# Batch 0 of a linear attention brought into the token-major form of the other batches, with the denominator put in the a factor, and a new hand order of the whole kernel

## The chip, the cores and the metric

The kernel runs on one core of one Trainium2 chip. The metric is the device time of one launch in microseconds (us), the median of several runs. The core has a matmul engine (PE, with its weight loads shown as PEld), a vector engine (DVE), a scalar engine (ACT), a general engine (POOL) and an engine that only issues transfers (SP). ACT and POOL can issue transfers too. Each engine works through its own list of instructions in the order in which the program wrote them, and waits at an instruction until what it reads is there.

## The reference: what is computed

Four batches of four heads, 1088 tokens of 32 dimensions each. Queries and keys are projected by S1 and S2 to two factors a and b of 8 numbers, whose outer product is a feature vector of 64. Attention is linear in these features; then comes a layer of width 2048 over all 4352 tokens.

```python
def phi(x):
    a = np.einsum('rd,bhsd->bhsr', S1, x)
    b = np.einsum('rd,bhsd->bhsr', S2, x)
    return np.einsum('bhsi,bhsj->bhsij', a, b).reshape(*x.shape[:-1], r * r)
q_p, k_p = (phi(q), phi(k))
kv = np.einsum('bhsf,bhsd->bhfd', k_p, v)
z = np.sum(k_p, axis=2)
num = np.einsum('bhsf,bhfd->bhsd', q_p, kv)
den = np.einsum('bhsf,bhf->bhs', q_p, z)[..., None] + 1e-06
attn = num / den
...
h = x @ w_in                                  # x: 4352 x 128, the heads side by side
g = h * (1.0 / (1.0 + np.exp(-beta * h)))
out = g @ w_out                               # 2048 -> 128
```

## The kernel before, in words

**The layer (W and V).** beta is multiplied into w_in (`prep_win`, L272) and 1/beta into w_out (`prep_wout_act`, L289, on ACT), so that a plain Silu does for g. The tokens go in ten chunks (`tok_chk`, L61: two of 256, seven of 512, one of 256). `w1` (L344), called W here, does one *wave* of a chunk: two matmuls of 512 tokens, or four of 256, into one of two PSUM tiles (L354), and one Silu of 128x1024 on ACT (L363) that writes g. `w2` (L318), called V, multiplies a g by its part of w_out and adds up in PSUM (L328); with a chunk's last wave DVE turns the sum (L338) and it is stored (L308). There are 68 waves, eight in a chunk of 512 and four in one of 256. V always takes the oldest g that no V has taken yet (`second`, L376), so by how many waves V lags behind W is set by the order in which both are called.

**Attention.** k and q are turned by DVE (L389 and L395) to have the dimension on the partitions. For batches 1 to 3 the work is *token-major*: `kps` and `qps` (L423, L428) project by S1 and S2 on PE, DVE turns the result back to tokens (`turn_ab`, L433), outer products on POOL and DVE make the features (`outer`, L447), `kv` (L498) sums v times features on PE over nine tiles, the features of k are summed to z on DVE (`sum_z`, L557) and added by matmuls on ones (`zs_mm`, L546). kv and z are spread on ACT and turned on PE (`nd_pe`), the features of q are turned by DVE (`turn_qo`, L460), `den_g` (L644) and `num_g` (L656) give denominator and numerator on PE, DVE inverts and spreads the denominator (`invert`, `spread_rc`, L585 to L598) and multiplies while it writes x (`divide_g`, L670). Batch 0 goes another way, in two pieces A and B: `spread` (L469) has PE project q with each a and b repeated so that a plain product (`mult`, L490) gives the features already turned, and z comes from a small Gram matrix of a and b (`gram`, L511, `gram_terms`, `gram_z`).

**Start.** The tiles of S1 and S2 and beta are loaded on ACT's queue (L102, L106), all the rest on SP's, in the order L167 to L179. Eleven matmuls on a constant tile keep PE at work meanwhile (L186).

**Order.** Every engine's list follows one list of short names, written by hand (`SEQ`, L850 on). In it W is `first` (L372), which makes a wave only if its tokens' x is written, and V is `second`, which does nothing without a g. What is left after the list is done by `rest(3)` (L380) with V three waves behind W. The PSUM tiles: two for waves (also used by projections and num), a double one ("two"), two single ones ("one", and "moeout", which holds V's sum; some chunks use "one" for it).

Of the kernel before, what the change touches and what calls it, by code (L numbers as in the profile page):

```python
# [14 lines left out]
P = 128  # L15
# [3 lines left out]
def kernel(  # L19
# [23 lines left out]

    NJK = 9
    TH = T // 2
    TPAD = 4 * NJK
    TCH = 512
    assert T == 34


    q_chk = [(0, 8), (16, 9)]
    QW = 32 * 9

    QB = [0, 9, 16, 25]
    JW = 32 * NJK
    JR = [(0, 2), (2, 4), (4, 6), (6, 9)]
    JR0 = [(0, 2), (2, 4), (4, 6), (6, 8), (8, 9)]
    WARM0 = 11
    NU = NJ // 2
# [7 lines left out]
    sbG = ctx.enter_context(tc.tile_pool(name="sbG", bufs=14))  # L67
# [23 lines left out]


    beta4 = sb([P, DFF // 4], F32, "beta4")
    beta_pu = sb([P, 2, NU], F32, "beta_pu")
    w_in_sb = sb([P, DFF], F32, "w_in_sb")
    w_out_sb = sb([P, NJ, P], F32, "w_out_sb")
    idle = sb([P, P], F16, "idle")
    nc.vector.memset(idle, 1.0)  # L98
    sr = []
    for n, s_ in enumerate((S1, S2)):  # L100
        t = sb([P, D], F32, f"sr{n}")
        nc.scalar.dma_start(  # L102
            out=t, in_=bass.AP(tensor=s_.tensor, offset=s_.offset, ap=[[0, P // R], [D, R], [1, D]])
        )
        sr.append(t)
    nc.scalar.dma_start(  # L106
        out=bass.AP(
            tensor=beta4.tensor,
            offset=beta4.offset,
            ap=[[32 * beta4.ap[0][0], 4], [1, DFF // 4]],  # L110
        ),
        in_=moe_beta.rearrange("(r c) -> r c", r=4),
    )
    nc.gpsimd.dma_start(
        out=beta_pu,
        in_=bass.AP(
            tensor=moe_beta.tensor, offset=moe_beta.offset, ap=[[NU, P], [P * NU, 2], [1, NU]]
        ),
    )
    k_t, q_t, v_t = {}, {}, {}  # L120

    def load_rows(src, dst, b, tag, parts=((0, T),)):
        if b not in dst:
            dst[b] = ld.tile([P, T, D], F32, tag=tag, name=tag)
        for t0, t1 in parts:
            nc.sync.dma_start(
                out=dst[b][:, t0:t1, :],
                in_=bass.AP(
                    tensor=src.tensor,
                    offset=src[b, 0].offset + t0 * D,  # L130
                    ap=[[T * D, P], [1, (t1 - t0) * D]],
                ),
            )


    def load_v(b):
        t = v_t[b] = ld.tile([P, H, NJK, D], F32, tag="v", name="v")
        if b == B - 1:
            nc.gpsimd.memset(t[96:, :, NJK - 2 :, :], 0.0)
        for g in range(4):  # L140
            nj = NJK if b < B - 1 else min(NJK, T - NJK * g)
            nc.sync.dma_start(
                out=t[32 * g : 32 * g + 32, :, :nj],
                in_=bass.AP(
                    tensor=v.tensor,
                    offset=v[b, 0].offset + NJK * g * D,
                    ap=[[T * D, 32], [S * D, H], [1, nj * D]],
                ),
            )

    def load_win(c0, c1):
        nc.sync.dma_start(out=w_in_sb[:, c0:c1], in_=moe_w_in[:, c0:c1])

    def load_wout(i):
        nc.sync.dma_start(
            out=w_out_sb[:, NU * i : NU * i + NU, :],
            in_=bass.AP(
                tensor=moe_w_out.tensor,
                offset=moe_w_out.offset + i * NU * P * P,
                ap=[[NU * P, P], [1, NU * P]],  # L160
            ),
        )

    K_PARTS = ((0, 18), (18, T))
    QA0 = 2 * q_chk[0][1]
    load_rows(k, k_t, 0, "k", K_PARTS)
    load_rows(q, q_t, 0, "q", ((0, QA0),))  # L167
    load_v(0)
    load_win(0, DFF // 2)
    load_wout(0)  # L170
    load_rows(q, q_t, 0, "q", ((QA0, T),))
    load_win(DFF // 2, DFF)
    load_rows(k, k_t, 1, "k")
    load_wout(1)
    load_rows(q, q_t, 1, "q")
    load_v(1)
    load_rows(k, k_t, 2, "k")
    load_rows(q, q_t, 2, "q")
    load_v(2)  # L179


    kvz0 = pso.tile([P, TCH], F32, tag="moeout", name="kvz")

    def keep_warm(n, fresh=False):
        for _ in range(n):
            nc.tensor.matmul(  # L186
                out=kvz0[:, P:],
                lhsT=idle,
                rhs=cut(idle, [[0, 3], [1, P]]),
# [5 lines left out]
    ones = sb([P, P], F32, "ones")  # L195
    nc.vector.memset(ones, 1.0)
    silu0 = sb([P, 1], F32, "silu0")
    nc.scalar.activation(out=silu0, in_=ones[:, :1], func=ACTF.Silu)
    ident = sb([P, P], F32, "ident")
    make_identity(nc, ident)  # L200

    hm = sb([P, 2, R], F32, "hm")
    nc.vector.memset(hm, 0.0)
    for h in range(H):
        nc.vector.memset(hm[32 * h : 32 * h + 32, h % 2, :], 1.0)
    gm = sb([P, 4], F32, "gm")
    nc.vector.memset(gm, 0.0)
    for c in range(4):
        nc.vector.memset(gm[32 * c : 32 * c + 32, c : c + 1], 1.0)
    e3 = sb([P, 3], F32, "e3")  # L210
    nc.vector.memset(e3, 0.0)
    nc.vector.memset(e3[:, 1:2], 1.0)

    mk = sb([P, H, R], F32, "mk")
    nc.gpsimd.tensor_tensor(
        out=mk,
        in0=cut(ident, [[2 * R, H], [1, R]]),
        in1=cut(ident, [[2 * R, H], [1, R]], 64),
        op=mybir.AluOpType.add,
    )  # L220

    kT2, qT2 = [], []
    for n in range(2):
        qT2.append(sb([P, T, 32], F32, f"qT{n}"))
        kT2.append(sb([P, TPAD, 32], F32, f"kT{n}"))
        nc.gpsimd.memset(kT2[n][:, T:, :], 0.0)
    zb0 = sb([P, H, 32], F32, "zb0")
    nc.gpsimd.memset(zb0, 0.0)
    zbg = []
    for n in range(2):  # L230
        t = sb([P, H, 2, 32], F32, f"zbg{n}")
        nc.gpsimd.memset(t, 0.0)
        zbg.append(t)

    keep_warm(WARM0, True)

    sk = sb([P, 2, 2, R], F32, "sk")
    skc = sk.rearrange("p m n r -> p (m n r)")
    sab = []


    def prep_s(n):
        st_ = sb([P, 4, R], F32, f"st{n}")
        nc.vector.transpose(out=st_.rearrange("p u r -> p (u r)"), in_=sr[n])
        nc.gpsimd.tensor_tensor(out=sk[:, :, n, :], in0=st_[:, :2, :], in1=hm, op=MUL)  # L245
        t = sb([P, R, R], F32, f"s{n}")
        nc.scalar.copy(out=t, in_=cut(st_, ([[1, R], [0, R]], [[0, R], [1, R]])[n]))
        sab.append(t.rearrange("p i j -> p (i j)"))


    beta_bc = sb([P, DFF], F32, "beta_bc")

    def beta_half(i):
        t = two("betaps")
# [3 lines left out]
        PS["beta", i] = t  # L258

    def beta_copy(i):  # L260
        nc.scalar.copy(  # L261
            out=beta_bc[:, 1024 * i : 1024 * i + 1024],
            in_=PS["beta", i].rearrange("p a b -> p (a b)"),
        )

    winp = sb([P, NJ, P], F16, "winp")
    woutp = sb([P, NJ, P], F16, "woutp")
    rbeta = sb([P, NJ], F32, "rbeta")

    given = set()  # L270

    def prep_win(j0, n, eng):  # L272
        for j in range(j0, j0 + n):
            given.add(j)
        i, u = divmod(j0, NU)
        o = i * (DFF // 2) + u
        eng.tensor_tensor(  # L277
            out=winp[:, j0 : j0 + n],
            in0=cut(w_in_sb, [[1, n], [NU, P]], o),
            in1=cut(beta_bc, [[1, n], [NU, P]], o),  # L280
# [3 lines left out]
    def prep_rbeta():  # L284
        nc.vector.reciprocal(out=rbeta, in_=beta_pu.rearrange("p i u -> p (i u)"))

    scaled = set()

    def prep_wout_act(j):  # L289
        scaled.add(j)  # L290
        nc.scalar.activation(  # L291
            out=woutp[:, j, :], in_=w_out_sb[:, j, :], func=ACTF.Copy, scale=rbeta[:, j : j + 1]
        )

    xT = sb([P, NTOK], F16, "xT")


    ALT = {len(tok_chk) - 3, len(tok_chk) - 1}
    moe = {"ci": 0, "w": 0, "ready": 0, "acc": None, "todo": []}
# [18 lines left out]
    def w2(ci, j0, jn, g):  # L318
# [6 lines left out]
        for jj in range(jn):  # L325
# [4 lines left out]
                lhsT=woutp[:, j, :],  # L330
# [13 lines left out]
    def w1():  # L344
        ci = moe["ci"]
        t0, tw = tok_chk[ci]
        per = TCH // tw
        jn = 2 * per
        j0 = moe["w"] * jn
        wv = psm.tile([P, 2, TCH], F32, tag="wave", name="wave")  # L350
        for jj in range(jn):
            assert j0 + jj in given
# [3 lines left out]
                lhsT=winp[:, j0 + jj],  # L356
# [5 lines left out]
        gw = per * tw  # L362
        nc.scalar.activation(out=g[:, :, :gw], in_=wv[:, :, :gw], func=ACTF.Silu)  # L363
# [8 lines left out]
    def first():  # L372
        if moe["ci"] < len(tok_chk) and sum(tok_chk[moe["ci"]]) <= moe["ready"]:
            w1()

    def second():  # L376
        if moe["todo"]:
            w2(*moe["todo"].pop(0))

    def rest(lag):  # L380
        while moe["ci"] < len(tok_chk):
            w1()
            if len(moe["todo"]) > lag:
                second()
        while moe["todo"]:
            second()

# [13 lines left out]
    PS, KP, QO, QT, QP, ND, KAB, QAB, ASB, KVZ, KVD, RB = ({} for _ in range(12))  # L401

    def wave2(name):
        return psm.tile([P, 2, 512], F32, tag="wave", name=name)

    def two(name):
        return ps2.tile([P, 2, 512], F32, tag="two", name=name)

# [484 lines left out]
```

## Time and profile before

| what | us |
|---|---|
| median of 3 runs | 116.27 (116.01 to 116.77) |
| profiled execution: span, the only time given for it | 111.9 |
| median less span | 4.4 |
| first W starts | 22.18 |
| x of batch 0 complete | 32.1 |
| W's start of the last 21 waves | 87.33 |
| ACT's 68 Silus, sum of busy time | 65.0 |
| ACT's 16 scalings of w_out | 5.3 |
| PE's matmuls of W and of V, sums of busy time | 39.4 and 37.3 |

The span runs from the first instruction to the last. The profile names an instruction by engine and line; L354 is W, L363 the Silu, L328 V. The mean time of one matmul there holds its whole way through the array; back to back, two of 512 columns take 0.43 us in the chain that ended last. An idle time is put down to the instruction that ended it. The granted clock of PE is given as a share of full speed: it is 1.00 in the first 7 us, changes between 0.5 and 1.0 up to 21 us, and is 1.00 from there.

### The profile page before, as it was taken

How to read it: one execution, taken by the hardware profiler on the slowest of the kernel's cores; microseconds unless marked ns; L12 is line 12 of the kernel's file. 1: busy time of each engine (PE TensorE's matmuls, PEld its weight loads, DVE VectorE, ACT ScalarE, POOL GpSimd, SP SyncE). 2: the span in 40 equal slices, each digit the busy share in tenths (PEclk: the TensorE clock that was granted, in tenths of full speed). 3: DMA queues.
4: the chain of work that ended last, by engine and by line, in shares of the span. 5: the costliest groups of instructions: out<-in, count | busy, mean ns of one | idle time of the engine just before them, and what ended most of it. 6: DMA issues, size and time to landing. Idle time of an engine off the chain costs nothing.

```text
span 111.9 us, 2866 instructions
## 1 busy us (share of the span) xinstructions
PE 100.7 (90%) x1167; PEld 47.9 (43%) x1167; DVE 70.2 (63%) x131; ACT 77.0 (69%) x99; POOL 35.2 (32%) x42
## 2 busy tenths in 40 slices
PE   6539998889999999989999999999899799999950
PEld 3214446234576643333564433344444344444630
DVE  3345727697796998999979779799919320020210
ACT  0503324697997796199899637689983599999930
POOL 5404928996995000070392007600000000000000
PEclk9985955799999999999999999999999999999999
DMA  3989999996002550007601471410150006014054
GB/s 91 298 160 287 415 419 244 253 292 130 18 5 40 78 179 6 0 7 108 187 0 17 60 182 40 74 26 0 15 81 4 0 0 94 6 18 64 15 82 59
DMA packets 22900, 11.33 MB, mean 101 GB/s; under 512 B 19028, under 2 KB 21092, under 8 KB 22888
## 3 DMA queue, kind: packets, MB, share of 16 engines
q1 hardware_dynamic: 22016, 11.05, 41.1%
q10 hardware_dynamic: 840, 0.11, 0.6%
q8 instruction: 9, 0.15, 0.5%
q14 instruction: 3, 0.02, 0.1%
q0 software_dynamic: 32, 0.01, 0.1%
HBM read 8.93 MB, written 2.23 MB: 100 GB/s over the span
## 4 chain that ended last, share of the span: by engine, by line
PE 79%; ACT 9%; DMA 5%; issue 1%; DVE 1%; ACTq 1%; POOL 0%
PE moeout L328 26%; PE wave L354 25%; ACT g L363 7%; PE kvz L501 5%; DMA sr<-in_S_dram 5%; PE nps L661 4%; PE kps L417 3%; PE dps L647 3%; PE betaps L257 2%; PE aps L477 2%; PE nps L605 2%; PE ndps L570 1%; PE kvz L186 1%; PE qps L417 1%; ACT woutp L291 1%
## 5 line engine op out<-in xcount | busy, mean ns | idle before, releaser
L363 ACT ACTIVATE g<-wave 128x1024 f16<-128x1024 f32 x68 | 65.0, 1040 | 14.8 <-PE wave L354 14.7
L354 PE MATMUL wave<-xT,winp 128*128 128x512 f16 (+1 forms) x160 | 39.4, 347 | 2.0 <-ACT g L363 1.6
L328 PE MATMUL moeout<-g,woutp 128*128 128x512 f16 (+1 forms) x160 | 37.3, 347 | 0.5 <-ACT g L363 0.4
L354 PEld LDWEIGHTS <-winp 128*128 128x128 f16 x160 | 14.4, 97 | 20.9 <-issue 12.8
L453 POOL TENSOR_TENSOR kp<-kab 128x512 f32<-128x512 f32 (+2 forms) x12 | 14.4, 1219 | 24.5 <-DVE kab L438 16.1
L328 PEld LDWEIGHTS <-woutp 128*128 128x128 f16 x160 | 15.2, 97 | 15.0 <-issue 2.6
L338 DVE STREAM_TRANSPOSE o_sb<-moeout 128x512 f32<-128x512 f32 (+1 forms) x10 | 6.3, 632 | 19.3 <-PE moeout L328 19.2
L277 POOL TENSOR_TENSOR winp<-w_in_sb,beta_bc 128x256 f16<-128x256 f32 x8 | 9.7, 1252 | 2.5 <-ACT beta_bc L261 2.5
L453 POOL TENSOR_TENSOR qo<-qab 128x512 f32<-128x512 f32 (+1 forms) x6 | 7.9, 1341 | 5.3 <-DVE qab L438 5.3
L464 DVE STREAM_TRANSPOSE qt<-qo 128x512 f32<-128x512 f32 (+1 forms) x12 | 8.9, 759 | 0.6 <-POOL qo L453 0.5
L186 PE MATMUL kvz<-idle 128*128 128x384 f16 x16 | 5.6, 472 | 1.1 <-DVE idle L98 1.1
L501 PEld LDWEIGHTS kvz<-kp,v 128*32 128x32 f32 x288 | 5.2, 123 | 2.8 <-issue 2.8
L417 PE MATMUL kps<-kT,sk 64*32 64x288 f32 x64 | 3.6, 482 | 3.0 <-POOL sk L245 3.0
L587 DVE STREAM_TRANSPOSE dT<-dps 128x288 f32<-128x288 f32 (+1 forms) x5 | 2.3, 468 | 6.2 <-PE dps L647 3.3
L501 PE MATMUL kvz<-kp,v 128*32 128x64 f32 x288 | 6.2, 239 | 0.0
L597 DVE STREAM_TRANSPOSE rb<-rc 128x576 f32<-128x576 f32 (+1 forms) x9 | 5.9, 685 | 0.2
L291 ACT ACTIVATE woutp<-w_out_sb,rbeta 128x128 f16<-128x128 f32 x16 | 5.3, 397 | 0.0
L390 DVE STREAM_TRANSPOSE kT<-k 128x1088 f32<-128x1088 f32 (+2 forms) x5 | 5.3, 1060 | 0.0
L396 DVE STREAM_TRANSPOSE qT<-q 128x1088 f32<-128x1088 f32 (+2 forms) x5 | 5.2, 1043 | 0.0
L661 PE MATMUL nps<-qt,nd 32*32 32x288 f32 x192 | 4.8, 412 | 0.0
L672 DVE TENSOR_TENSOR xT<-nps,rb 128x576 f16<-128x576 f32 x6 | 4.4, 737 | 0.3
L453 DVE TENSOR_TENSOR qo<-qab 128x512 f32<-128x512 f32 (+1 forms) x6 | 4.5, 758 | 0.0
(72 smaller groups left out, 76.4 us busy)
## 6 DMA issues: line engine op xcount, KB each, us to landing
v<-in_v_dram SPq DMA_DIRECT2D x15, 144.0 KB, 6.4
k<-in_k_dram SPq DMA_DIRECT2D x3, 544.0 KB, 7.4
q<-in_q_dram SPq DMA_DIRECT2D x3, 544.0 KB, 11.7
w_in_sb<-in_moe_w_in_dram SPq DMA_DIRECT2D x2, 512.0 KB, 5.5
w_out_sb<-in_moe_w_out_dram SPq DMA_DIRECT2D x2, 512.0 KB, 7.5
out_dram<-o_sb SPq DMA_DIRECT2D x16, 64.0 KB, 2.0
out_dram<-o_sb SPq DMA_DIRECT2D x10, 32.0 KB, 1.7
k<-in_k_dram SPq DMA_DIRECT2D x1, 288.0 KB, 3.0
```

The source lines that it names most:

```text
L186: nc.tensor.matmul(out=kvz0[:, P:], lhsT=idle, rhs=cut(idle, [[0, 3], [1, P]]), start=fresh, stop=True, skip_group_check=True,)
L277: eng.tensor_tensor(out=winp[:, j0 : j0 + n], in0=cut(w_in_sb, [[1, n], [NU, P]], o), in1=cut(beta_bc, [[1, n], [NU, P]], o), op=MUL,)
L291: nc.scalar.activation(out=woutp[:, j, :], in_=w_out_sb[:, j, :], func=ACTF.Copy, scale=rbeta[:, j : j + 1])
L328: nc.tensor.matmul(out=moe["acc"][:, :tw], lhsT=woutp[:, j, :], rhs=g[jj], start=(j == 0), stop=(j == NJ - 1),)
L338: nc.vector.transpose(out=o_sb[:, :nt, :].rearrange("p t d -> p (t d)"), in_=moe["acc"][:, :tw])
L354: nc.tensor.matmul(out=wv[:, jj // per, o : o + tw], lhsT=winp[:, j0 + jj], rhs=xT[:, t0 : t0 + tw], start=True, stop=True,)
L363: nc.scalar.activation(out=g[:, :, :gw], in_=wv[:, :, :gw], func=ACTF.Silu)
L417: nc.tensor.matmul(out=t[32 * g : 32 * g + 32, pi, :JW], lhsT=skc[rows, :], rhs=moving(rows, g), start=True, stop=True,)
L453: (eng or nc.vector).tensor_tensor(out=cut(dst[b][:, j0:j1], [[F, n], [R, R], [1, R]]), in0=cut(a0, [[2 * R, n], [1, R], [0, R]]), in1=cut ...
L464: nc.vector.transpose(out=QT[b][:, j0:j1].rearrange("p j h c s -> p (j h c s)"), in_=QO[b][:, j0:j1].rearrange("p j h f -> p (j h f)"),)
L501: nc.tensor.matmul(out=KVZ[b][32 * h : 32 * h + 32, :F], lhsT=v_t[b][:, h, j, :], rhs=KP[b][:, j, h, :], start=(j == 0), stop=(j == NJK - ...
L661: nc.tensor.matmul(out=tiles[g // 2][32 * h : 32 * h + 32, g % 2, :JW], lhsT=ND[b][rows, fc, 32 * h : 32 * h + 32], rhs=QT[b][rows, :, h, ...
```

## The change

It does seven things.

1. All attention is token-major. Batch 0 goes in three pieces A, B, C of 8, 8 and 18 tiles of 32 tokens (`Q_PART`: first tile of each of four groups, and tiles per group; C's groups overlap), with q projected, turned and multiplied as in the other batches.
2. The denominator is q's a times c, where c is q times W', and W' is S2's transposed Gram: a small Gram matrix of a and b of k for every batch (nine matmuls, `gram`), copied by ACT, multiplied by S2 on the diagonal blocks (`w_prime`) and masked by DVE (`w_mask`). c is four matmuls (`q_c`), turned by DVE. DVE forms a times c, sums over eight, inverts, and multiplies the a factor by that before the outer product (`den_mul`, `den_inv`, `den_a`). The sums of the features, the denominator's matmuls, the spread of its inverse, and the product at x's writing go away; `put_x` copies num to x.
3. The layer's weights are prepared in four quarters in place of eight pairs: w_in and w_out are loaded in four parts each, POOL multiplies w_in by beta in four instructions, and the prepared weights lie as [c][u], so that one weight load reads every fourth element.
4. The tile of S1 leads SP's queue and that of S2 ACT's. ACT also issues, behind the table load and a first Silu, the second part of k of batch 0, beta, and two quarters of w_in. SP issues the rest.
5. The copies of beta to SBUF are four halves (`beta_copy`) on ACT; the broadcast be0 stands ahead of k's projection on PE.
6. W and V are unconditional: `first` and `rest` are gone, W is `w1` itself, and V takes the oldest g. All 68 of each are written in the list.
7. The buffers of g are 12, not 14. k and q of each batch are turned in two parts, k's outer products cut in five (2, 2, 2, 2, 1 tiles).

The core of the diff:

```diff
-    q_chk = [(0, 8), (16, 9)]
+    Q_PART = {"A": ([0, 2, 4, 6], 2), "B": ([8, 10, 12, 14], 2), "C": ([16, 21, 24, 29], 5)}
+    for b in range(1, B):
+        Q_PART[str(b)] = (QB, NJK)
...
-    sbG = ctx.enter_context(tc.tile_pool(name="sbG", bufs=14))
+    sbG = ctx.enter_context(tc.tile_pool(name="sbG", bufs=12))
...
-                lhsT=winp[:, j0 + jj],
+                lhsT=winp[:, j // U, :, j % U],
...
-    def first():
-        if moe["ci"] < len(tok_chk) and sum(tok_chk[moe["ci"]]) <= moe["ready"]:
-            w1()
     def second():
-        if moe["todo"]:
-            w2(*moe["todo"].pop(0))
-    def rest(lag):
...
+        w2(*moe["todo"].pop(0))
...
+    def gram(b):
+        t = PS["gram", b] = one("gram")
+        for j in range(NJK):
+            c = 32 * (j % 4)
+            nc.tensor.matmul(out=t[c : c + 32, : H * R], lhsT=KAB[b][:, 1, j], rhs=KAB[b][:, 0, j], ...)
+    def w_prime(b):
+        nc.tensor.matmul(out=PS["gram", b][:, 2 * H * R : 3 * H * R], lhsT=s2bd, rhs=PS["gsb", b], ...)
+    def w_mask(b):
+        nc.vector.tensor_tensor(out=t, in0=cut(PS["gram", b], ...), in1=cut(gm, ...), op=MUL)
+    def q_c(nm, bank):
+        for g in range(4):
+            nc.tensor.matmul(out=t[32 * g : 32 * g + 32, : 32 * n], lhsT=PS["wbd", b],
+                             rhs=qT[:, st0[g] : st0[g] + n, :], start=True, stop=True)
+    def den_mul(nm, eng):
+        eng.tensor_tensor(out=tmp[n][:, :, :, :R], in0=QAB[nm][:, 0], in1=CC[nm], op=MUL)
+    def den_inv(nm):
+        nc.vector.tensor_reduce(out=RD[nm], in_=tmp[n], axis=mybir.AxisListType.X, op=mybir.AluOpType.add)
+        nc.vector.reciprocal(out=RD[nm], in_=RD[nm])
+    def den_a(nm, eng):
+        eng.tensor_tensor(out=t, in0=QAB[nm][:, 0], in1=cut(RD[nm], ...), op=MUL)
...
+    DO = {"m": masks, "ts": turn_s, "rb": prep_rbeta, "W": w1, "V": second}
...
     SEQ = """
+        ls0s ls1a m lk0.0s lk0.1a lqAs lb4a lv0s li0a lo0s lbpg li1a lo1s lqBs li2s lo2s li3s lo3s lqCs lk1s
+        lq1s lv1s mW ts msD m2P tk00 tk01 be0 kp0t bc00A bc01A be1 bc10A bc11A h h tqA ka00 ka01 qpAw qtA gr0
+        gc0A rb o00D o01P o02D wp0 wm0 kv00 kv01 cpAo ctA h kv02 dmAD diA daAD o03D o04P kv03 kv04 wi0P ns0A
+        pA0D tA0 nt0 nc0A nAww xA0A xA1A wi1P wa0 wa1 W wa2 wa3 tqB wi2P wi3P W V qpBt qtB wa4 wa5 W wa6 wa7
+        cpBo ctB dmBD diB daBD V W wa8 wa9 wa10 wa11 pB0D tB0 V nBtw wa12 wa13 wa14 wa15 xB0D xB1D V W tqC qpCt
+        qtC W V cpCo ctC dmCD diC daCD V W pC0D tC0 pC1P V W tC1 pC2D tC2 V nCtw xC0A xC1D lk2s lq2s lv2s tk10
+        tk11 kp1t W V ka10 ka11 o10P o11P gr1 gc1A W V wp1 wm1 tq10 tq11 W V qp1t cp1o qt10 qt11 ct1 dm1D di1
+        da1D W V o12D o13D o14P p10P p11D t10 W V t11 kv10 kv11 p12P t12 W V kv12 kv13 kv14 ns1A p13D p14P t13
+        t14 W V nt1 nc1D W V n1tw x10D x11D W V lk3s lq3s lv3s tk20 tk21 kp2t W V ka20 ka21 o20P o21P gr2 gc2A W
...
+        t33 t34 W V nt3 nc3D W V n3tw x30D x31D W W W W W W V W V W V W V W V W V W V W V W V W V W V W V W V W
...
     """
     for s_ in SEQ.split():
         DO[s_]()
-    rest(3)
```

How the names in the list read: a letter s, a or g at the end of a load (l...) names the queue, SP's, ACT's or POOL's; D, P or A at the end of others DVE, POOL or ACT. tk and tq turn k and q; kp and qp project them; ka and qt turn the projections; o and p are the outer products of k and q, t the turns of the latter; gr, gc, wp and wm are Gram, its copy, W' and its mask; cp and ct are c and its turn; dm, di and da the three steps of the denominator; kv sums, ns, nt and nc spread, turn and copy its result; n is num and x its copy to x; be and bc broadcast beta and copy it; wi and wa prepare w_in and w_out; h is one keep-warm matmul. Batch 2's and batch 3's parts of the list repeat batch 1's, with one more W V pair between x21 and tk30.

## The prediction

> **What bounds the kernel now.** I read the page's head, the list of waits, the chain that ended last, ACT's timeline and, for the clock, a table by stretches. First the shares (page, part 1):
>
> ```profile
> span 111.9 us, 2866 instructions
> PE 100.7 (90%) x1167; PEld 47.9 (43%) x1167; DVE 70.2 (63%) x131; ACT 77.0 (69%) x99; POOL 35.2 (32%) x42
> ```
>
> PE is nearly always occupied, DVE and ACT two thirds of the time. The list of waits tells how W (two or four L354 matmuls and ACT's Silu g of L363) and V (the L328 matmuls that read g) mesh:
>
> ```profile
> ACT g L363 <- PE wave L354: 14.7, 18, 3.1
> ...
> PE wave L354 <- ACT g L363: 1.6, 5, 0.6
> ...
> PE moeout L328 <- ACT g L363: 0.4, 1, 0.4
> ```
>
> In 68 waves V waited for its g once, for 0.4 us: each V takes a g that was made a few waves before. The chain shows what one g costs when PE does wait for it, and the tail behind it:
>
> ```profile
> 85.07 0.54 PE wave L354 x2
> 85.61 1.73 PE moeout L328 x8
> 87.33 0.45 PE wave L354 x2
> 87.78 0.02 issue
> 87.80 0.02 ACTq L363
> 87.82 0.04 issue
> 87.86 1.03 ACT g L363
> 88.89 0.04 issue
> 88.94 0.59 PE wave L354 x2
> ```
>
> ```profile
> 87.86 19.35 ACT L363 ACTIVATE g<-wave 128x1024 f16<-128x1024 f32 x21 [1.14 <-PE wave L354]
> 108.38 0.90 ACTq L308 DMA_DIRECT2D out_dram<-o_sb  x2
> ```
>
> From a W's start (87.33) to the first PE work behind its g (88.94) are 1.61 us; two V matmuls take 0.43. Once attention is done, the last 21 waves go at 19.35/21 = about 0.92 us each. W's start at 87.33 to the span's end at 111.9 is 24.6 us: 21 x 0.92 and 5.3 fixed (first W, last V, turn, store). Hence a tail of n waves costs 5.3 + 0.917 n.
>
> **The sum's base.** The page gives the profiled execution no other time than its span, 111.9 us. The median of the runs is 116.27, so 4.4 us (3.9%) lie around the instructions; I keep them unchanged.
>
> **The change, part by part.**
>
> *The order of W and V.* The old list skips a W whose x is missing and lets V lag; the new one writes every W and V. I counted both along the new list. Before nC (last piece of batch 0) there are 8 W and 8 V: nothing is left to consume. From there to n3 each W is followed at once by the V of the same wave: 8 pairs up to n1, 9 from n1 to n2, 10 from n2 to n3, 27 in all. PE runs matmuls in list order, so at each V it stands until its own g is ready, and behind it queue the next kps, gram, W', qps, kv or num, for which DVE then waits. The cost of a pair: first W behind an attention matmul 0.54 to 0.55 instead of 0.45 (85.07 row), so 1.61 + 0.1 + 0.43 = 2.14 us, against 0.92 in the tail: 1.2 us more, 27 times, 33 us. The rest of the waves, 33 (old 21), follow n3 as tail. There six W go ahead, so V lags again.
>
> *Attention matmuls of a batch of 1 to 3.* Kept: kps 0.65, qps 0.65, kv 1.2 (72 instructions, 1.14 to 1.28), num 1.53. Removed: den (1.11), z's matmuls on ones (0.11 to 0.16), two of four turns. Added: c = q W' with four instead of eight calls, 0.55 (half of den's 1.11); gram for every batch, 18 instructions, which took 0.96 at half clock, so 0.3 to 0.9, I take 0.5; W', one 128x128 f32 matmul, from the turn rows 0.3 (0.2 to 0.5). Two turns 0.35. Sum 5.73, against about 6.0 before: no gain worth a tenth of what the pairs cost. The ends give 5.4 to 6.3 a batch, +-1.5 over three.
>
> *DVE.* Removed per batch: sums of kp (1.2 + 0.7 + 0.4 + 0.4), spread of 1/den (1.44). Added: product with c, reduction, 1/x, a times 1/den (0.42, 0.4, 0.38, 0.42 by the 128x256 and 128x36 rows; the reduction is in no row, 0.3 to 0.75 between 128x256 and 128x512 products). x becomes a copy at the divide's 0.74. About 15 us per batch, below the 25 that follow for PE. DVE stands at wm some 4 us, for W' is behind a pair; then q's turn (1.4) fits under the next pair (2.14), the chain c, den, a, products and turns ends some 3 us before num needs it. So its own costs are nothing here, covered by the pairs' holds; without these holds DVE would bound (rival 2).
>
> *Where the hold is replaced:* after x1 of batch b, kps waits for x (1.5) and k's turn (1.35). In batch 1 no pair lies there: 2.0 us (C's x is smaller). In batch 2 one pair covers all but 0.9, in batch 3 two cover all.
>
> Batch 1: 8 x 2.14 + 5.73 + 2.0 = 24.9. Batch 2: 9 x 2.14 + 5.73 + 0.9 = 25.9. Batch 3: 10 x 2.14 + 5.73 = 27.1. Sum 77.9.
>
> *Batch 0.* The S tiles lead two queues; the second was the old start's holder (1.45 to 6.79 in the chain). But ACT issues k's second part behind its table load (1.28) and silu, at about 3.0 instead of 1.2, so with 3.7 to landing it is there at 6.7; and on PE be0 stands ahead of kps, waiting for beta, issued on ACT at 3.5 to 4.5 (landing unseen; POOL's beta took 3.9): 7.5. With PE idle from 4.4, the clock is at half as before from 7.2. be0 1.4, kps 1.48 end at 10.4 (before 8.86). Then, end by end, at the rows' durations of this half clock: be1 and two keep-warm matmuls 12.5, q's projection 12.9, its turns 13.5, gram 13.9, its copy 14.2, W' 14.8, wm (behind rb, o00 and o02 on DVE, 0.24 + 0.7 + 0.7) 15.6, c 16.0, turn, product, sum, 1/x and a on DVE (0.2 to 0.25 each) 17.4, o03 18.1, the last kv 18.7, spread on ACT 19.2, turn 19.7, nd 20.2, num A (64 matmuls, 1.1 to 1.5) 21.6, x on ACT 22.3: first W at 22.4, where it was (22.18). Part B: from here ACT does 16 scalings at 0.32 to 0.35 (5.3 in both kernels) among five g, and V1 to V3 each wait for the four scalings of their quarter (24.7, 27.9, 31.3); num B stands behind V3 and ends at 32.9, xB at 33.6. Part C: q's turn 34.8, projection behind W5 35.1, its turns 35.9, c behind W6 and V5 36.4, den and a 38.1, products and turns (2 x 0.7, 0.7, 2 x 0.42) 41.0, while W and V alternate on PE; V8 41.3, num 1.2: nC ends at 42.5, where before the whole of batch 0 was divided by 32.1. Ends: 36 (be0 not late, scalings hidden) to 46.
>
> *Weights read with step 4.* winp becomes [c][u]; its weight load reads every fourth f16. The contiguous load takes 97 ns under a 214 ns matmul. No row has a step; the longest load is zc's, 221 ns (64 columns, f32, half clock). Ends: 0 and (221 - 97) x 27 = 3.3 for pairs, plus up to 48 x (221 - 107) = 5.5 in the 256 wide waves. Below 0 isn't possible, since the load is hidden now. I take 0, since the row nearest in type and size is the 97. The Trainium skill, "TensorE: Matmul & The Clock Gate", section "Weight-path perf modes", has the fast load work for column steps from -1,023 to 1,024, by which this is 0 too; no run here shows it.
>
> *Hidden:* 2 KB rows of w_in and w_out instead of 4 KB, and preparation on POOL in four: the loads fill the DMA engines till some 22 us in both, and the last quarter is needed at 25. The 8 issues of w and the loads on SP precede any store. Cover gone, a late quarter would move W1 by its lateness.
>
> Sum: 42.5 + 77.9 = 120.4 at n3's end; + 5.3 + 33 x 0.917 = 35.6: span 156.0; + 4.4 = **160.4 us**.
>
> **Rivals.**
>
> 1. *The clock falls in the pairs.* The granted clock changed at 7.2, 10.7, 14.1 and 21.0 us, so I took stretches of 3.4:
>
> ```profile
> 7.20:10.65 3.45, 3.27 (x41) 0.52 0.86 211
> 10.65:14.10 3.45, 3.45 (x57) 0.99 1.01 402
> 14.10:17.50 3.40, 3.40 (x45) 0.51 1.03 414
> ...
> 86.00:89.40 3.40, 2.81 (x14) 1.00 0.00 0
> ```
>
> (Columns: stretch, length, PE busy, clock, DMA share, GB/s.) It fell at 14.1 though PE was never idle, after a stretch of small f32 matmuls; from 21 on it stayed whole, with PE busy at least about three quarters. In a pair PE is busy 1.18 of 2.14, 55%. So whole clock isn't shown for that, nor loss. At half clock a pair is 0.95 longer (W 0.46, V 0.43, start) and attention's 5.73 near 11: 27 x 0.95 + 3 x 5 = 40 us, 200 if throughout; a third to half of the time 174 to 180. The skill's same page, section "A second HAM failure mode", has short idle gaps between matmul groups at N=512 make the clock swing; by it this rival would hold. Chance 0.24.
>
> 2. *V holds nothing,* because g comes early enough: then pairs take 0.92 and DVE sets the batch, about 15 plus the wait at wm, 17.5: 42.5 + 52.5 + 35.6 + 4.4 = 135. Against it: the chain at 87.33 shows 1.61. Chance 0.03.
>
> 3. *Batch 0 is done early,* nC at 36: 154. Chance 0.12.
>
> 4. *Faster,* the other side: one mechanism, the pairs cost nothing extra and n3 ends soon. To reach 116.3, 44.1 of 160.4 us must go, 1.63 of each pair's 2.14; left 0.51, less than its 0.86 of matmuls. From 12 us a batch it would decide; DVE alone has 15. Chance 0.01.
>
> **How the numbers follow.** Forecast 0.60, the rivals 0.24, 0.03, 0.12, 0.01. The forecast's own range, from batch 0 (-4 to +4), attention (+-1.5) and weights (0 to +8), is 154 to 170. The 8 in 10 range takes in most of rival 3 and the milder half of rival 1: 151 to 182. All but rival 4 are slower by over 1%, which is about what a measurement of this kernel can tell: faster 0.01, same 0.01, slower 0.98.
>
> **What would show it.** Right: PE moeout waiting for ACT g 27 times, some 1.1 us each (30 us in the list of waits), ACT at under half in the batches, n3 near 120, 33 g in one run at the end at 0.92 each. Wrong: V's waits below 10 us in sum; DVE busy without a gap in the batches; L354 weight loads near 200 ns; a clock row below 1.00 after 40 us (rival 1); first W later than 25.

## The result and the profile after

| | us |
|---|---|
| before, median of 4 runs beside the changed kernel | 116.14 (115.27 to 116.77) |
| after, median of 4 runs | 175.21 (171.58 to 185.71) |
| ratio, 95% interval | 1.486 [1.468, 1.504] |
| profiled execution after: time, span, mean granted clock | 171.58, 169.7, 0.87 |
| the other three: spans, with mean granted clock | 171.8 (0.93), 174.5 (0.88), 183.6 (0.74) |

The change costs 59 us by the medians. The ratio, here and in the experiments, takes only runs within 1.5% of the fastest of their kernel (here 171.58 and 173.89 after), while the medians take all. The longest run is the one with the lowest granted clock, which will be a part of the answer, though the shortest, at 0.87, isn't the one with the highest. First the head of the page after, with the line of the granted clock in 40 slices of 4.2 us:

```profile
span 169.7 us, 3182 instructions
PE 116.4 (69%) x1310; PEld 52.6 (31%) x1310; DVE 73.5 (43%) x148; ACT 78.4 (46%) x102; POOL 31.5 (19%) x39
...
PEclk9955559999999999695699999658795879999998
```

PE fell from 90% to 69% of a span that is half as long again, and no other engine took its place: everyone waits. From slice 17 on (68 us) the clock is no longer always whole. Whom PE waits for stands in the list of waits (who for whom: us in total, times, longest):

```profile
ACT g L369 <- PE wave L361: 59.8, 38, 4.2
...
PE moeout L333 <- ACT g L369: 34.1, 31, 1.2
...
DVE wbd L459 <- PE gram L448: 14.1, 3, 5.2
```

V waited for its g once before, for 0.4 us; now 31 times, 1.1 us each. Four of these lie in batch 0, 27 in the batches 1 to 3, one for each written pair. The first line is the other half of the picture: ACT, which makes the g's, waits for W too, 59.8 us in all. The chain that ended last shows a pair with an attention step of PE ahead:

```profile
51.54 0.65 PE qps L400 x16
52.18 0.62 PE cps L473 x8
52.81 0.57 PE wave L361 x2
...
53.40 1.03 ACT g L369
...
54.47 0.59 PE moeout L333 x2
55.06 0.45 PE wave L361 x2
```

W, g and V stand one behind the other, with no other PE work under the 1.03 us of the Silu. A pair lasts 2.25 us here (52.81 to the next W at 55.06), against 0.92 for a wave of the tail. The table by stretches, cut at the ends of n of batch 0 (nC), 1, 2 and 3 (columns: stretch, length, busy time of PE, PEld, DVE, ACT and POOL, granted clock, DMA share, GB/s):

```profile
41.50:67.10 25.60, 14.71 (x230) 6.30 (x231) 15.20 (x26) 9.15 (x11) 6.95 (x7) 1.00 0.28 73
67.10:97.60 30.50, 19.14 (x237) 7.15 (x236) 16.24 (x28) 9.78 (x11) 6.65 (x6) 0.83 0.27 68
97.60:130.60 33.00, 21.28 (x239) 7.87 (x240) 16.20 (x27) 10.80 (x12) 6.59 (x6) 0.80 0.08 14
130.60:169.70 39.10, 32.22 (x150) 15.55 (x148) 4.83 (x7) 30.94 (x33) 0.00 (x0) 0.94 0.18 31
```

DVE has the same 15 to 16 us of work in each batch, about half of it; no engine is full. The second and third batch hold one pair more than the one ahead, some 2.2 us, yet the second is 4.9 longer than the first: their clock is 0.83 and 0.80, which by 2 x (1 - clock) x length is some 24 us at half clock.

### The profile page after: what moved, and what is told of

Its sections match the earlier page's. It is cut to its first block, busy times and chain, and to the rows that moved or that the text cites. A ratio compares the mean times of both kernels' runs of the same rounds, so it can differ in the third digit from the quotient of the medians.

```text
span 169.7 us, 3182 instructions
## 1 busy us (share of the span) xinstructions
PE 116.4 (69%) x1310; PEld 52.6 (31%) x1310; DVE 73.5 (43%) x148; ACT 78.4 (46%) x102; POOL 31.5 (19%) x39
## 4 chain that ended last, share of the span: by engine, by line
PE 62%; ACT 24%; DVE 6%; issue 3%; DMA 2%; ACTq 1%; DVEq 0%
PE moeout L333 23%; ACT g L369 22%; PE wave L361 21%; PE nps L588 5%; PE kvz L548 3%; PE qps L400 3%; DMA beta<-in_moe_beta_dram 2%; PE kps L400 2%; PE cps L473 2%; PE betaps L265 2%; DVE kp L516 2%; DVE o_sb L343 1%; PE kvz L564 1%; DVE xT L602 1%; PE gram L433 1%
## 5 line engine op out<-in xcount | busy, mean ns | idle before, releaser
L369 ACT ACTIVATE g<-wave 128x1024 f16<-128x1024 f32 x68 | 66.8, 1041 | 60.0 <-PE wave L361 59.8
L333 PE MATMUL moeout<-g,woutp 128*128 128x512 f16 (+1 forms) x160 | 43.9, 371 | 36.7 <-ACT g L369 34.1
L361 PE MATMUL wave<-xT,winp 128*128 128x512 f16 (+1 forms) x160 | 44.7, 379 | 3.4 <-ACT g L369 2.1
L516 POOL TENSOR_TENSOR qo<-qa,qab 128x512 f32<-128x512 f32 (+1 forms) x10 | 13.4, 1363 | 47.7 <-DVE qa L507 47.7
L516 POOL TENSOR_TENSOR kp<-kab 128x512 f32<-128x512 f32 (+1 forms) x11 | 9.7, 910 | 39.5 <-DVE kab L410 39.5
L602 DVE CAST xT<-nps 128x576 f16<-128x576 f32 (+2 forms) x9 | 5.5, 624 | 12.2 <-PE nps L588 10.8
L516 DVE TENSOR_TENSOR kp<-kab 128x512 f32<-128x512 f32 x9 | 9.6, 1102 | 0.0
L588 PE MATMUL nps<-qt,nd 32*32 32x288 f32 (+2 forms) x384 | 8.9, 391 | 0.5 <-ACT nd L576 0.5
L516 DVE TENSOR_TENSOR qo<-qa,qab 128x512 f32<-128x512 f32 (+1 forms) x10 | 9.0, 903 | 0.1
L459 DVE TENSOR_TENSOR wbd<-gram,gm 128x32 f32<-128x32 f32 x4 | 0.8, 188 | 14.1 <-PE gram L448 14.1
L385 DVE STREAM_TRANSPOSE kT<-k 128x576 f32<-128x576 f32 (+1 forms) x8 | 5.6, 726 | 1.2 <-DMA k<-in_k_dram 1.2
L276 POOL TENSOR_TENSOR winp<-w_in_sb,beta_bc 128x512 f16<-128x512 f32 x4 | 5.8, 1488 | 0.0
```

Of the source, the lines that this page charges most:

```text
L276: eng.tensor_tensor(out=winp[:, n].rearrange("p c u -> p (c u)"), in0=w_in_sb[:, o : o + FQ], in1=beta_bc[:, o : o + FQ], op=MUL,)
L333: nc.tensor.matmul(out=moe["acc"][:, :tw], lhsT=woutp[:, j // U, j % U, :], rhs=g[jj], start=(j == 0), stop=(j == NJ - 1),)
L361: nc.tensor.matmul(out=wv[:, jj // per, o : o + tw], lhsT=winp[:, j // U, :, j % U], rhs=xT[:, t0 : t0 + tw], start=True, stop=True,)
L369: nc.scalar.activation(out=g, in_=wv, func=ACTF.Silu)
L516: eng.tensor_tensor(out=cut(o, [[F, n], [R, R], [1, R]]), in0=cut(a, [[R, n], [1, R], [0, R]]), in1=cut(b_, [[R, n], [0, R], [1, R]]), op=MUL,
L588: nc.tensor.matmul(out=t[g // 2][32 * h : 32 * h + 32, g % 2, : 32 * n], lhsT=ND[b][rows, fc, 32 * h : 32 * h + 32], rhs=QT[nm][rows, :, h ...
```

## Experiments

Theory: the time is lost where V follows its own W; any lag brings it back. Rivals: the new attention form itself (longer chains on DVE and PE), the halved clock, the thin batches and the long tail.

**One: the same list with V three waves behind W** (e1_lag3), and **one wave behind** (e5_lag1).

```diff
-  ... tk10 tk11 kp1t W V ka10 ka11 o10P o11P gr1 gc1A W V wp1 wm1 tq10 tq11 W V qp1t ...
+  ... tk10 tk11 kp1t W ka10 ka11 o10P o11P gr1 gc1A W wp1 wm1 tq10 tq11 W qp1t ...
...
-  V V V V V V
+  V V V V V V V V V
```

With a lag of one only the first of these three V moves.

> The changed kernel with one thing altered in its order: the first three V of batch 1 are left out there and stand at the end of the list, so that V takes a g three waves old all through batches 1 to 3. Theory (PE stands at each V for its own g, 27 times some 1.15 us, and the low load of PE that comes of it lets the clock fall): 27 x 1.35 = 36 us and the half-clock losses (about 10) go, PE no longer bounds the batches, DVE does at some 18 to 20 us each; about 41.5 + 3 x 19 + 39 + 2 = 130 to 140 us, PE's waits for g under 5 us in sum, clock 1.00 from 45 us on. Rival (the waits at V are covered by DVE's work, and the token-major form and the hand order bound): within 5 us of the changed kernel's 175.

> The changed kernel with one V of batch 1 left out there and put at the end of the list: V takes a g one wave old through batches 1 to 3. Theory (a hold of 1.15 us comes only of taking the g of the same wave): the g of the wave before is there at least 1.4 us after its W, so the holds shrink to under 0.3 and the time lies within 3 us of the kernel with V three waves behind (149.7). Rival (three waves are needed, since ACT falls behind where it also copies): halfway, 158 to 165.

Measured: three waves 149.71 us (148.73 to 150.85; 1.308 [1.290, 1.326] of before), one wave 152.43 (1.333 [1.306, 1.361]). V's waits for g fell to the line below in the first, all of it in batch 0, and to 3.9 us in the second, 1.2 of it in the batches:

```profile
PE moeout L333 <- ACT g L369: 2.7, 4, 1.1
```

So moving three V by hand is worth 25 us, and one wave of lag gives 23 of it. The 27 holds had 31.4 (34.1 less 2.7 for batch 0's four). The 25 hold some clock as well, since the batches run at 1.00, 1.00 and 0.94 here; experiment three takes the clock alone. And 33 us over the kernel before stay, more than the theory had. In this run a batch lasts 19.6, 21.0 and 23.4 us, and the chain through them has gone over to DVE: 38 us of it lie there and 22 on PE, where in the changed kernel 2 us lay on DVE. A part from the first batch:

```profile
54.73 2.08 DVE kp L516 x2
56.80 1.48 DVE qo L516
58.28 1.81 DVE qt L538 x3
```

Of the profiled spans' difference (148.4 less 111.9, 36.5 us), cut at the ends of n in both, 13.9 lie in batch 0 (44.1 against 30.3), 9.2 in the batches (64.0 against 54.8), 13.4 in the tail (40.3 against 26.8), which holds 33 waves in place of 22. The first of these is loose: nC ended between 41.5 and 46.0 us in the profiled executions of five kernels with the very same list up to there (the changed kernel, e1_lag3, e2_spread, e5_lag1, e6_overlap).

**Two: the old kernel with the new kernel's coupling** (e3_before_nolag). From `va1` (batch 1's kv) to the end of the list each W takes its V at once; the attention is the old one.

```diff
...
     def first():
         if moe["ci"] < len(tok_chk) and sum(tok_chk[moe["ci"]]) <= moe["ready"]:
             w1()
+            if hold["on"]:
+                while moe["todo"]:
+                    second()
...
     for s_ in SEQ.split():
+        hold["on"] = hold["on"] or s_ == "va1"
         DO[s_]()
+    hold["on"] = False
     rest(3)
```

> The kernel before with one part of the change alone: from batch 1's kv on, until the list ends, each W is followed at once by every V that is due, so V has no lag in some 37 waves; attention, loads and the tail are as before. Theory (no lag is the main cost, in whatever form attention is done): 37 x 1.35 = 50 us less the some 5 to 9 us that PE idled for waves before, so 155 to 170 us if the clock stays whole, up to 185 if it falls as in the changed kernel. Rival (the new attention form and DVE's waits are the main cost): under 130.

Measured: 191.83 us (189.05 to 194.45; 1.658 [1.625, 1.690]), 76 us more with nothing else changed. The waits, the engines and the clock:

```profile
PE moeout L328 <- ACT g L363: 41.1, 36, 1.2
```

```profile
PE 137.2 (71%) x1167; PEld 55.9 (29%) x1167; DVE 71.6 (37%) x131; ACT 79.1 (41%) x99; POOL 35.5 (18%) x42
...
PEclk9855559999996555555755599555855555899999
```

The profiled execution (194.45 us, the longest of the four) has a span of 192.5 us, 80.6 over that of the kernel before. 36 holds of 1.14 us are 41 of these. The clock was about half for most of 54.6 to 160 us (0.60 in the mean), and the same 1167 matmuls kept PE busy for 137.2 us in place of 100.7: 36.5 more. The holds do this without the new attention, and the clock lost with them weighs nearly as much as they do. That is more than was expected.

**Three: the holds filled, so that the clock stays** (e4_fill): the changed kernel with three matmuls on zeros ahead of each V of batches 1 to 3 that isn't its chunk's first. They add nothing to the sum.

```diff
...
+        if j0 and fill["on"]:
+            for _ in range(3):
+                nc.tensor.matmul(out=moe["acc"][:, :tw], lhsT=idle,
+                                 rhs=cut(zeros, [[0, tw // P], [1, P]]), start=False, stop=False)
...
```

> The changed kernel with three matmuls of a constant by zeros (512 columns) put ahead of each V of batches 1 to 3 that isn't the first of its chunk; they add zero to V's sum and need no g, so they run while PE would stand. Theory (the half-clock stretches between 69 and 138 us come from PE's low load): 3 x 0.21 = 0.64 us fit into each 1.15 us hold, the pairs stay at 2.25, the clock stays 1.00 from 30 to 130 us, and the some 10 us lost to half clock come back: span near 158, time 160 to 164, and less scatter between runs. Rival (the clock goes by something else, or full rows alone don't count): clock falls as often as before and the time stays within 3 us of 172 to 176; if the fillers delay V, it is longer.

Measured: 167.19 us (166.60 to 171.57; 1.458 [1.440, 1.477]): 8 us less than the changed kernel by the medians, with 69 extra matmuls, but less than was expected (160 to 164). The runs that the ratios take have means of 167.0 and 172.7, 5.7 us apart, and the two intervals overlap a little, so the gain rests on the stages as well. In the profiled execution, batch by batch:

```profile
45.83:74.25 28.42, 22.50 (x253) 9.22 (x252) 15.20 (x26) 9.17 (x11) 6.95 (x7) 0.81 0.24 65
74.25:102.00 27.75, 21.45 (x258) 8.82 (x257) 16.10 (x27) 9.76 (x11) 6.64 (x6) 0.94 0.30 74
102.00:130.75 28.75, 22.23 (x268) 9.44 (x267) 16.10 (x27) 10.79 (x12) 6.58 (x6) 1.00 0.09 16
```

At clocks of 0.94 and 1.00 the last two batches take 56.5 us, where they took 63.5. The first lost: it was at half clock from 44 to 57 us and took 28.4 in place of 25.6, and as nC came 4.3 later too, this execution (171.57 us) was no shorter than the profiled one of the changed kernel. Some 7 us of the changed kernel's time is clock, read from two batches of one execution each. The Trainium skill, "TensorE: Matmul & The Clock Gate", section "A second HAM failure mode", tells of a clock that swings when PE pauses often and briefly between groups of matmuls; the two tables agree with it.

**Four: where the rest is.** e2_spread takes e1_lag3 and moves 13 waves from the tail into batches 2 and 3. e6_overlap instead puts the k part of the next batch, half of its outer products and q's turn into the batch before; it keeps the lag and has 23 waves in the tail.

```diff
-  o12D o13D o14P p10P p11D t10 W V t11 kv10 kv11 p12P t12 W V kv12 ...
+  o12D o13D o14P qt10 qt11 ct1 dm1D di1 da1D p10P W V tk20 tk21 kp2t p11D t10 p12P W V ka20 ka21 gr2 gc2A ...
```

> As the kernel with V three waves behind, and 13 of the 33 waves of the tail are moved ahead: 7 more W V into batch 2 and 6 into batch 3, the most that x allows. Theory (with the hold gone, PE has room in batches 2 and 3 beside DVE's work, and each wave taken from the tail saves up to 0.92 us there): batches 2 and 3 go to 16 x 0.92 + 5.7 = 20.4 us of PE, so they grow by at most 2 each, the tail shrinks by 12: 8 to 12 us faster than the kernel with V three behind alone. Rival (PE or ACT is full in the batches already, each moved wave costs there what it saves): within 3 us of it.

> V three waves behind as before, and the batches overlapped: k's turn, projection, Gram, W' and mask of the next batch, half of its outer products and its q's turn stand inside the batch before; 14 to 15 waves stand in batches 2 and 3, 23 in the tail. Theory (what is left of the slowdown without the hold is that a batch is one serial chain over DVE and PE, about 20 to 28 us long, and the next starts only behind its x): batches fall to 17 to 20 us, since DVE has some 16 us of work each, 44 + 57 + 29 + 2 = 130 to 136. Rival (DVE or PE is full in the batches): no better than 146.

Measured: e2_spread 148.35 us (147.96 to 149.75; 1.298 [1.282, 1.313]), only 1.4 less than e1_lag3: the tail fell from 40.3 to 27.1 us, batches 2 and 3 rose from 44.4 to 56.5. Waves moved into a batch cost there what they saved: each of the batch's seven steps on PE stands behind two waves in the list, and DVE's listed waits for PE in the two batches rise from 12.8 to 22.3 us. Besides, V stood 4.2 us in one place till DVE, busy with products, turned the chunk's sum ahead of it. e6_overlap 141.37 us (141.31 to 142.31; 1.250 [1.238, 1.262]): with other attention work beside the chain, batches with 14 or 15 waves take 22.0 and 20.9 us. It is between the 130 to 136 of the theory and the 146 of its rival.

**Five: batch 0's head.** e7_overlap_head is e6_overlap with be0 and be1 behind the projections and V three behind from the first W; e8_few_waves is that with 9 waves each in batches 2 and 3 and 34 in the tail.

```diff
-  tk00 tk01 be0 kp0t bc00A bc01A be1 bc10A bc11A h h tqA ka00 ka01 qpAw qtA gr0 gc0A rb ...
+  tk00 tk01 kp0t be0 bc00A bc01A tqA ka00 ka01 qpAw qtA gr0 gc0A be1 bc10A bc11A rb ...
```

> The overlapped kernel, and in batch 0 the broadcasts of beta stand behind the projections on PE (the two keep-warm matmuls there are left out), and V lags three waves from the first W on. Theory (be0 holds kps for 1.1 us, and V's holds in B and C put nC back by some 3): 3 to 5 us faster than the overlapped kernel. Rival (DVE's chain bounds batch 0): within 1.5 us of it.

> The kernel with the head altered and batches overlapped, but only 9 waves each in batches 2 and 3, and 34 in the tail. Theory (beside DVE's 16 us a batch PE has room for some 11 waves, the rest lengthens the batch as much as it shortens the tail): batches 2 and 3 near 17, total within 4 us of the one with 14 and 15 waves. Rival (waves in the batches are free): 10 us slower than that.

Measured: e7_overlap_head 141.55 us (140.00 to 144.44; 1.245 [1.227, 1.263]), no gain. nC ended at 41.6 in place of 44.3, but batch 1 took 27.2 in place of 23.1: between k's turn of batch 1 and that of batch 2 DVE stands for 6.3 us in place of 2.1, which is the whole difference; 2.4 of it is the wait for the sum of a V that now falls due inside batch 1, ahead of k's products in DVE's list, and the rest goes with a clock of 0.50 from 41 to 46 us, 1.00 in e6_overlap. The profiled execution was the longest of the four (144.44), but e8_few_waves, with the same list that far, has the same 27.3 us and 6.3 of standing. Its nC ended at 37.7, 3.9 ahead of e7_overlap_head's with the same head, so 2.7 earlier in one execution shows little. e8_few_waves took 146.38 us (144.42 to 146.93; 1.287 [1.266, 1.307]), 5 more, between its theory (within 4) and its rival (10). Batches 2 and 3 fell to 19.0 and 17.2 us, 6.7 less than in e7_overlap_head, and the tail rose from 30.6 to 41.1: filling the batches pays once attention overlaps.

**Six: w_in without the step** (e9_contig): e6_overlap with the weights as [u][c] again.

```diff
-    winp = sb([P, NB, P, U], F16, "winp")
+    winp = sb([P, NB, U, P], F16, "winp")
...
-                lhsT=winp[:, j // U, :, j % U],
+                lhsT=winp[:, j // U, j % U, :],
```

> This is the kernel of the run with the batches overlapped (e6_overlap, 141.37 us), with the prepared w_in lying as [u][c] again, so that the weight load of W reads neighbours in place of every fourth element; POOL's four multiplications read with a step instead. Nothing else differs. In e6_overlap a strided load took 111 to 113 ns and V's contiguous one 97, both under matmuls of some 215 ns. Theory (the step costs nothing, as the prediction chose): loads of W at 97 ns, time within 1 us of 141.4, unless POOL's four instructions become longer (1.49 us each before) and make the first W late. Rival (the loads are not all hidden, the prediction's upper end): up to 27 x 0.015 for waves behind a hold plus the 96 narrow matmuls, 1 to 2 us less, 139.5 to 140.5.

Measured: 144.51 us (143.53 to 146.33), 3 more than e6_overlap. By medians that is 1.255 of the kernel before (115.12), where e6_overlap has 1.225 (141.37 and 115.39). First its loads, then those of e6_overlap (ns: least, median, most):

```profile
L361 PEld LDWEIGHTS <-winp x160: 95/98/151, 25.0 to 136.2; 128*128 128x128 f16 x160
```

```profile
L361 PEld LDWEIGHTS <-winp x160: 111/113/152, 22.2 to 131.6; 128*128 128x128 f16 x160
```

The step costs 15 ns a load. Time it doesn't cost: from the end of n of batch 1 on, with the clock at 1.00 in both executions, batches 2 and 3 and the tail take 22.0, 20.9 and 28.9 us with either load. The column-step rule that the prediction named ("TensorE: Matmul & The Clock Gate", "Weight-path perf modes", of the Trainium skill) doesn't say that a stepped load is as short, and it isn't quite.

The 3 us more come ahead of that. Reading with the step moved to POOL's preparation, which went from 1.49 to 2.72 us for each quarter, 5.8 to 9.5 us together, and DVE's products of batch 0 beside it took longer: k's first two 3.82 us in place of 2.44, the two of the denominator 0.96 and 1.67 in place of 0.26 and 0.62. The first W came 2.8 us later, at 25.57. That POOL holds DVE up here is read from these times and not tested by itself; the last section has more of it.

## Why the prediction was right, and where its sizes were off

The direction and the mechanism were right, and 175.2 us lies in the range of 151 to 182. The forecast, 160.4, was 14.8 below, and its own range, 154 to 170, was missed: what saved the number is the half of rival 1 that the wider range took in. The profiled execution, point by point:

| end of | predicted | measured | own error |
|---|---|---|---|
| batch 0 (nC) | 42.5 | 41.5 | -1.0 |
| batch 1 | 67.4 | 67.1 | +0.7 |
| batch 2 | 93.3 | 97.6 | +4.6 |
| batch 3 | 120.4 | 130.6 | +5.9 |
| span | 156.0 | 169.7 | +3.5 |
| around the span | 4.4 | 1.9 | -2.5 |

- *The holds.* "PE moeout waiting for ACT g 27 times, some 1.1 us each": 27 in the batches. e1_lag3 and e3_before_nolag show them from both sides. The forecast that they hold nothing (rival 2) is out: without lag they cost, with the clock that goes with them, 25 us here and 76 in the old kernel.
- *A pair at 2.14 us.* It measured 2.2 to 2.3 at whole clock (2.20 to 2.32 in e4_fill). V's two matmuls take 0.59 until the next work when PE stood idle ahead of them, not 0.43. Over 27 pairs some 3 to 4 us: the first term that was too small.
- *The clock.* This is the step that failed. The sum took whole clock, with 0.24 for rival 1, which had half clock for a third to half of the time and 174 to 180 us. The sign that the prediction gave for it, a clock row below 1.00 after 40 us, came: of the 89 us of the batches about 24 were at half clock. That the time lies in rival 1's stretch is partly luck: the fall was milder, by e4_fill the clock itself gives some 7 us, and the pair's and the tail's errors made up the rest. A pair at half clock takes 3.04 us in the chain of batch 2 (77.90 to 80.94), 0.90 more than the predicted 2.14, where 0.95 was reckoned:

```profile
77.90 0.87 PE wave L361 x2
...
78.86 1.03 ACT g L369
...
79.93 1.01 PE moeout L333 x2
80.94 1.14 PE qps L400 x16
```

- *The tail, 35.6 us.* It took 39.1. The first four W alternate with their g at 1.8 to 2.1 us (starts at 130.62, 132.51, 134.28 and 136.41), where 0.92 was reckoned, partly at half clock; and once V stands for DVE's turn of the sum (0.8 us). e4_fill's tail, mostly at whole clock, was 38.3, so only about 1 us of it is clock.
- *Batch 0.* The first W came at 21.5 (22.4 predicted) and nC at 41.5 (42.5); beta landed at 6.4, not 7.5, and k's projection ended at 8.2, not 10.4. Rival 3 (36) didn't come. That nC fits to 1.0 us is partly luck, since it ended at 41.5 to 46.0 us in five executions of the same list. That batch 0 is done some 10 us later than before was in the sum. Which part of its new form costs them wasn't settled.
- *DVE.* 15.2 to 16.2 us a batch, "about 15" predicted, and never the bound in the changed kernel. Its wait at wm was 14.1 us in three batches, 4.7 each ("some 4"). That without the holds DVE would bound is half right: in e1_lag3 the chain lies on DVE for 38 of 64 us, but DVE is busy for 47 of them, in turn with PE, and batches last 20 to 23 us rather than the 17.5 of rival 2.
- *Kept at nothing:* the stepped weight load, rightly (the stages of e9_contig). *Around the span:* 1.9 us in the profiled execution. The 4.4 came from setting a median of other runs against the span of one quick execution: a run of the kernel before that has this span of 111.9 us took 113.85.

## What to carry to other kernels

Where matmuls feed another engine's activation and later ones read its result, put at least one wave of other work between: one wave of lag was worth 23 us here, three 25. Counting the places where a list writes consumer right behind producer gives the number of holds, and one row of the trace the price. Then reckon the clock as well: a list of short idle gaps may leave PE at half clock, which cost some 7 us here and some 36 in the old kernel with the same holds. And a median isn't to be set against the span of a single execution.

## What the hardware showed that was not expected

**What load the clock asks for.** The granted clock changes on edges 3.413 us apart. Cut at those edges, the table by stretches of the changed kernel reads:

```profile
66.11:69.52 3.41, 1.61 (x50) 0.72 (x34) 2.52 (x5) 0.89 (x1) 0.00 (x0) 1.00 0.47 78
69.52:72.94 3.42, 3.12 (x20) 0.62 (x20) 1.36 (x3) 0.15 (x2) 0.00 (x0) 0.50 0.91 284
72.94:76.35 3.41, 1.45 (x22) 0.60 (x22) 0.00 (x0) 2.00 (x3) 2.69 (x3) 1.00 0.85 212
76.35:79.76 3.41, 2.13 (x6) 1.00 (x6) 1.47 (x3) 1.13 (x2) 0.00 (x0) 0.50 0.00 0
79.76:83.18 3.42, 3.25 (x27) 0.59 (x27) 0.85 (x2) 0.12 (x1) 0.00 (x0) 0.50 0.00 0
```

The windows after 1.61 and 1.45 us of busy PE are at half clock; there 3.12 us brings the whole clock back and 2.13 doesn't. I counted this over the 11 profiled executions of this case, from 20 us on (or from where the clock first shows an edge, 37 us at the latest). At whole clock a window with PE busy for less than 1.6 us was followed by half clock 28 times in 31, one with 1.6 to 2.0 us 5 times in 28, one with 2.0 or more never in 244. At half clock 3.0 us or more brought whole clock 34 times in 34, 2.8 to 3.0 three times in 6, less never in 40. A pair keeps PE busy for 1.18 of 2.25 us, 1.8 us of a window, so which windows fall depends on what attention work happens to lie between: batch 1 never fell, with its lowest at 1.73 until the last. This is a count and not a test; in the first 20 us the clock also fell behind a window in which PE was never idle, as the prediction's 10.65 row shows, and what set it off there is open.

**Products on DVE and POOL slow each other.** The groups of the changed kernel's products (ns: least, median, most):

```profile
L516 POOL TENSOR_TENSOR qo<-qa,qab x10: 1071/1450/1576, 37.1 to 119.1; 128x512 f32<-128x512 f32 x7, 128x256 f32<-128x256 f32 x3
L516 DVE TENSOR_TENSOR kp<-kab x9: 677/760/1757, 11.9 to 116.7; 128x512 f32<-128x512 f32 x9
```

A product of DVE takes 0.68 us alone and up to 1.76 beside one of POOL: longer by about what a POOL product takes alone (1.07). The Trainium skill, "SBUF — State Buffer", section "SBUF: two separate sides", has the two hold a shared pair of ports in turn, each for a whole instruction. DVE's least and most agree with it. The sum doesn't quite: from 55.34 to 59.47 three products of each, 4.8 us alone (3 x 0.68, 2 x 1.07, and 0.63 by the shortest of k's 256 wide ones), were done in 4.1.
